# Cutting the first weight load and the last one of a decode kernel into row groups and single rows

## The chip, the cores and the metric

The kernel runs on one core of one Trainium2 chip. The metric is the device time of one execution in microseconds (us); medians and ranges over several executions are quoted. A profile covers one execution. Its span, from the first to the last instruction, is about 1.7 us shorter than the device time of the same execution (1342.8 and 1344.51 us for the kernel before).

Terms of the views: PE is TensorE, DVE is VectorE, ACT is ScalarE, and SPq is the SyncE queue that issues the loads. HBM is the memory that the loads read, SBUF the on-chip memory of 128 partitions that they write. The chain of waits starts from the last instruction and goes back, at each step, to what released it. "issue" is time in which an engine waited for nothing that the profile shows.

## The reference

One decode step for 4 sequences with one new token each: attention over an 8192-long cache with 32 heads, mixed with a gated feed-forward block. Cut to what matters:

```python
q = x @ wq                                # wq: 1024 x 4096, bf16, 8 MB
scores = q . k_cache * Dh ** -0.5         # k_cache: 4 x 32 x 8192 x 128, 268 MB
o = softmax(scores) . v_cache             # v_cache: the same size
a = o @ wo                                # wo: 4096 x 1024, 8 MB
b = x + sigmoid(r) * ((silu(x @ w_gate) * (x @ w_up)) @ w_down)
return g * a + (1 - g) * b
```

Nearly all the work is to read the two caches once.

## The kernel before

All loads are issued by the SyncE queue (SP) into a ring of five slots in SBUF, each 32 KB for each of 128 partitions. `load_pair` fills two slots with one DMA where they are neighbours. The first load is wq: row c of the view is partition c, with 64 KB.

```python
def load_pair(src, n, apart=False):
    a = slots(2)
    if a + 1 < NS and not apart:
        lo = a * RING
        nc.sync.dma_start(out=flat[:, lo:lo + 2 * n], in_=src)
        return [flat[:, lo:lo + n], flat[:, lo + n:lo + 2 * n]]
    # ... two DMAs where the slots are not neighbours

N = H * Dh
wq_at = load_pair(A_wq.rearrange("(c t) n -> c (t n)", t=DT), DT // 2 * N)
# ... small loads of x, w_r and gate_w, then w_gate, K, V ...
```

A pass after scheduling, `begin_early`, moves the first DMA of the program ahead of the barrier at which the engines meet on entry. At the other end the last loads are blocks of wo. Each block is four rows of 1024 for each partition. The last two blocks are loaded in halves, so that TensorE can begin on a half:

```python
last = [wo_block(g) for g in range(2, NWB - 2)]
last += [wo_block(g, r, r + FR // 2) for g in (NWB - 2, NWB - 1) for r in (0, FR // 2)]
# ... each use() is two matmuls (one for each half of the output) for every row
```

## Time and profile before

| | before |
|---|---|
| median time | 1344.42 us (1344.25 to 1344.47, 3 runs) |
| profiled span | 1342.8 us |
| PE busy / DVE busy | 77% / 46% of the span |
| chain of waits, DMA's share | 65% |
| first load (wq) issued / landed | 0.00 / 22.1 us |

The page's slices cut the span into 40 equal parts of 33.6 us. "DMA" is the busy share of the 16 DMA engines in tenths, "GB/s" what they moved.

```profile
DMA  9999999999999999999999999999999999999997
GB/s 414 434 434 430 432 436 430 444 433 418 445 430 424 440 431 425 437 436 432 432 438 431 426 433 430 434 436 435 432 423 441 430 427 431 436 426 443 423 423 331
```

The DMA engines are full from the first slice to the last. So I reckon that time lost at the start of the stream is not won back later, and that time after the last landing is added.

The chain of waits of the first 80 us (start us, length us, what):

```profile
1.46 20.99 DMA x<-in_gate_w_dram
...
23.48 3.63 PE S_ps L313 x32
27.11 0.02 issue
27.13 0.33 SPq L198
27.45 16.35 another core or an unknown queue
43.81 0.02 issue
43.82 34.94 DMA ring<-in_A_k_cache_dram
```

The tiny loads of x, w_r and gate_w queue behind wq, so that they land at 22.4 us. TensorE computes q; that frees a slot for the second half of the first K load (27.13 us). The load after that is issued at 43.82 us. By the order of the ring it waits for a slot of w_gate; the chain does not name what released it. The loads in the queue bridge these waits.

The first PE groups in the timeline (start us, busy us, what; in brackets the idle time before and what ended it):

```profile
22.58 0.63 PE L226 MATMUL small<-identb,x 6*128 6x6 bf16 x8 [22.58 <-DMA x<-in_gate_w_dram]
23.48 5.36 PE L313 MATMUL S_ps<-ring,xw 128*4 128x512 bf16 x64 [0.28 <-DVE xw L228]
...
39.34 5.97 PE L313 MATMUL o_ps<-ring,xw 128*4 128x512 bf16 x56 [4.99 <-DMA ring<-in_B_w_gate_dram]
```

The end of the chain of waits, and the last PE groups of the timeline:

```profile
1323.81 15.04 DMA ring<-in_A_wo_dram
1338.85 0.04 issue
1338.89 1.04 PE acc L279 x4
1339.93 0.02 issue
1339.95 0.57 ACT TB L590
```

```profile
1333.72 3.71 PE L279 MATMUL acc<-ring,LT 128*4 128x512 bf16 x16 [0.33 <-DMA ring<-in_A_wo_dram]
1337.66 1.02 PE L279 MATMUL acc<-ring,LT 128*4 128x512 bf16 x4 [0.23 <-DMA ring<-in_A_wo_dram]
1338.89 1.02 PE L279 MATMUL acc<-ring,LT 128*4 128x512 bf16 x4 [0.21 <-DMA ring<-in_A_wo_dram]
```

TensorE waits about 0.2 us for each of the last two halves, and four matmuls follow the last landing.

The trace also records every packet of the load queue. The kept records do not name the engine. I put the wq packets in order of their start and cut them into rounds of 16, one for each DMA engine:

```
wq before, 64 KB packets: starts (us)   duration (us): mean, min, max
round 1                   1.01 to 1.80  3.20  2.89  3.44
round 2                   4.11 to 4.71  2.42  2.42  2.42
... (rounds 3 to 7: means 2.42 to 2.53)
round 8                  18.61 to 19.38 2.42  2.42  2.42    last end 21.79
```

After the first round a packet of 65,536 bytes takes 2.42 us in nearly every case, which is 27.1 GB/s for an engine, or 433 GB/s for 16.

### The profile page before, as it was taken

The page shows a single profiled execution, that of the slowest core. Times are in us where ns is not written, and L with a number is a line of the kernel's source. Part 1 is how long each engine was busy: PE and PEld are TensorE (multiplying, and loading weights), DVE is VectorE, ACT ScalarE, POOL GpSimd, SP SyncE. Part 2 cuts the span into 40 slices and gives each one's busy share as a digit, 9 for nine tenths or more (in the row PEclk, how much of TensorE's full clock was granted, in tenths as well). Part 3 has the DMA queues.
Part 4 walks back from the last instruction along what each step waited for, and adds up shares of the span by engine and source line. Part 5 has one row for each costly group of instructions (what it writes and reads, how often), then busy time and mean ns, then how long its engine had stood idle before and what let it go on. Part 6 is the DMA issues. An engine that isn't in the chain of part 4 may idle for free.

```text
span 1342.8 us, 7621 instructions
## 1 busy us (share of the span) xinstructions
PE 1033.8 (77%) x4536; PEld 226.1 (17%) x2348; DVE 612.4 (46%) x358; ACT 50.6 (4%) x46; POOL 55.3 (4%) x90
## 2 busy tenths in 40 slices
PE   2665877787788687778987779598778679877897
PEld 0111111111111111111211112111111112111221
DVE  2555655544346554335455546146555244556000
ACT  0000100001000010001000010000100010000100
POOL 2000010001000010001000010000100010000100
PEclk9687988988999898889888889898889799889799
DMA  9999999999999999999999999999999999999997
GB/s 414 434 434 430 432 436 430 444 433 418 445 430 424 440 431 425 437 436 432 432 438 431 426 433 430 434 436 435 432 423 441 430 427 431 436 426 443 423 423 331
DMA packets 14172, 576.18 MB, mean 429 GB/s; under 512 B 1582, under 2 KB 1590, under 8 KB 2108
## 3 DMA queue, kind: packets, MB, share of 16 engines
q1 hardware_dynamic: 14132, 575.69, 99.5%
q8 instruction: 27, 0.44, 0.1%
q14 instruction: 5, 0.04, 0.0%
q10 hardware_dynamic: 8, 0.00, 0.0%
HBM read 575.68 MB, written 0.01 MB: 429 GB/s over the span
## 4 chain that ended last, share of the span: by engine, by line
DMA 65%; DVE 20%; PE 12%; another core or an unknown queue 1%; ACT 0%; issue 0%; SPq 0%; DVEq 0%
DMA ring<-in_A_k_cache_dram 56%; DVE TB L443 20%; PE o_ps L523 10%; DMA ring<-in_A_v_cache_dram 7%; DMA x<-in_gate_w_dram 2%; DMA ring<-in_A_wo_dram 1%; PE S_ps L449 1%; ACT PB L494 0%; PE S_ps L313 0%; PE acc L313 0%; PE small L543 0%; ACT OS L535 0%; PE acc L279 0%; DVE OS L536 0%
## 5 line engine op out<-in xcount | busy, mean ns | idle before, releaser
L443 DVE STREAM_TRANSPOSE TB<-ring 128x2048 uint32<-128x2048 uint32 x256 | 567.3, 2278 | 495.2 <-DMA ring<-in_A_k_cache_dram 493.9
L449 PE MATMUL S_ps<-TB,Z 128*128 128x512 bf16 x2048 | 520.0, 409 | 218.7 <-DVE TB L443 218.5
L523 PE MATMUL o_ps<-ring,PB 128*32 128x512 bf16 x2048 | 461.9, 389 | 52.5 <-DMA ring<-in_A_v_cache_dram 47.9
L449 PEld LDWEIGHTS <-Z 128*128 128x128 bf16 x1024 | 105.5, 103 | 628.8 <-issue 627.3
L523 PEld LDWEIGHTS <-PB 128*32 128x32 bf16 x1024 | 100.9, 99 | 410.0 <-issue 401.3
L536 DVE SCALAR_TENSOR_TENSOR OS<-o_ps,mE,OS 128x512 f32<-128x512 f32 x8 | 6.0, 751 | 104.1 <-ACT OS L535 104.1
L474 ACT ACTIVATE PTs<-S_ps,negm 128x1024 bf16<-128x1024 f32 x8 | 8.9, 1114 | 1024.9 <-DVE negm L471 1024.9
L425 POOL TENSOR_TENSOR Z<-qa,mq 128x16 bf16<-128x16 bf16 x32 | 9.1, 286 | 744.4 <-PE S_ps L449 654.7
L496 POOL COPY PB<-PT 32x1024 bf16<-32x1024 bf16 x16 | 30.4, 1903 | 82.1 <-PE o_ps L523 81.7
L494 ACT COPY PB<-PT 32x1024 bf16<-32x1024 bf16 x16 | 30.5, 1907 | 1.5 <-DVE PT L476 1.3
L376 DVE CAST LT<-small 128x64 bf16<-128x64 f32 x2 | 0.5, 225 | 40.6 <-PE small L374 40.6
L226 PE MATMUL small<-identb,x 6*128 6x6 bf16 x8 | 0.6, 197 | 22.6 <-DMA x<-in_gate_w_dram 22.6
L467 POOL PARTITION_ALL_REDUCE gmx<-mex x8 | 3.2, 396 | 340.7 <-DVE mex L464 340.7
L462 DVE TENSOR_REDUCE m<-S_ps 128x1 f32<-128x1024 f32 x8 | 9.8, 1225 | 15.9 <-PE S_ps L449 15.9
L279 PE MATMUL acc<-ring,LT 128*4 128x512 bf16 x64 | 15.0, 378 | 2.0 <-DMA ring<-in_A_wo_dram 1.4
L476 DVE STREAM_TRANSPOSE PT<-PTs 128x1024 bf16<-128x1024 bf16 x8 | 10.0, 1245 | 10.2 <-ACT PTs L474 10.2
L279 PE MATMUL acc<-ring,hT 128*4 128x512 bf16 x56 | 12.2, 379 | 0.0
L535 ACT ACTIVATE OS<-o_ps,mE 128x512 f32<-128x512 f32 x8 | 5.5, 687 | 158.8 <-PE o_ps L523 158.8
L313 PE MATMUL o_ps<-ring,xw 128*4 128x512 bf16 x56 | 6.0, 555 | 5.0 <-DMA ring<-in_B_w_gate_dram 5.0
L543 PEld LDWEIGHTS small<-selg,OS 128*128 128x128 f32 x64 | 9.0, 208 | 4.1 <-issue 3.9
L543 PE MATMUL small<-selg,OS 128*128 128x16 f32 x64 | 8.7, 269 | 0.0
L548 DVE SCALAR_TENSOR_TENSOR OT<-small,sgb,rinv 128x16 bf16<-128x16 f32 x8 | 1.8, 225 | 10.5 <-PE small L543 10.5
(71 smaller groups left out, 67.1 us busy)
## 6 DMA issues: line engine op xcount, KB each, us to landing
ring<-in_A_k_cache_dram SPq DMA_DIRECT2D x14, 4096.0 KB
ring<-in_A_v_cache_dram SPq DMA_DIRECT2D x14, 4096.0 KB, 31.2
ring<-in_B_w_gate_dram SPq DMA_DIRECT2D x1, 7168.0 KB, 37.6
ring<-in_B_w_up_dram SPq DMA_DIRECT2D x1, 7168.0 KB, 39.2
ring<-in_B_w_down_dram SPq DMA_DIRECT2D x2, 3584.0 KB, 27.5
ring<-in_A_wo_dram SPq DMA_DIRECT2D x6, 1024.0 KB, 21.0
ring<-in_A_v_cache_dram SPq DMA_DIRECT2D x2, 2048.0 KB, 26.8
ring<-in_A_v_cache_dram SPq DMA_DIRECT2D x4, 1024.0 KB, 25.0
```

The source lines that it names most:

```text
L279: nc.tensor.matmul(out_ap, lhsT=lhsT, rhs=rhs, start=start, stop=True, skip_group_check=True)
L313: nc.tensor.matmul(ps[32 * k:32 * k + Bn, z, :], lhsT=xT[TW * half + t], rhs=cols(w, t, 4 * z + k), start=(half + t == 0), stop=(half == 1 ...
L425: nc.gpsimd.tensor_tensor(out=Z[:, :, QP - 1:QP - 1 + P].rearrange("p e (q c) -> p e q c", c=QP)[:, :, :, 0], in0=qa[:, :, h0:h0 + NQ, b], ...
L443: nc.vector.transpose(out=flat_t.bitcast(U32), in_=kn[:, c * CJ * Dh:(c + 1) * CJ * Dh].bitcast(U32))
L449: nc.tensor.matmul(sps[:, z, :], lhsT=Z[:, he, s:s + P], rhs=T[:, 16 * z:16 * z + 16, half, :, e], start=(t == 0 and n == 0 and he == 0), ...
L462: nc.vector.tensor_reduce(out=m1[:], in_=sps[:].rearrange("p z n -> p (z n)"), axis=AX.X, op=ALU.max)
L474: nc.scalar.activation(out=PTs[:], in_=sps[:].rearrange("p z n -> p (z n)"), func=ACT.Exp, bias=negm[:, 0:1], scale=scale, accum_out=rs[:, ...
L476: nc.vector.transpose(out=PT[:].rearrange("p j i -> p (j i)"), in_=PTs[:])
L494: nc.scalar.copy(out=Bv[at, :, :, q, :], in_=Pv[at])
L496: nc.gpsimd.tensor_copy(out=Bv[at, :, :, q, :], in_=Pv[at])
L523: nc.tensor.matmul(o_ps[row:row + NM, e, :], lhsT=PB[:, RD * t + c, z, w].rearrange("p e s j -> p (e s j)"), rhs=vn[:, j0 * Dh:(j0 + 4) * ...
L543: nc.tensor.matmul(oT[:, :], lhsT=o_sb[:, q * Dh:(q + 1) * Dh], rhs=selg[:, q].rearrange("p t s -> p (t s)"), start=(q == 0), stop=(q == 3))
```

## The change

The intent has two parts. At the start, a smaller first load could let every DMA engine get its first packet sooner: 16 rows, one for each engine, go ahead of the barrier, and the other 112 rows follow it. At the end, a smaller last load leaves TensorE less work after the last landing.

```diff
-    def load_pair(src, n, apart=False):
+    def load_pair(src, n, p0=0, p1=P, apart=False):
...
-            nc.sync.dma_start(out=flat[:, lo:lo + 2 * n], in_=src)
+            nc.sync.dma_start(out=flat[p0:p1, lo:lo + 2 * n], in_=src)
...
-    wq_at = load_pair(A_wq.rearrange("(c t) n -> c (t n)", t=DT), DT // 2 * N)
+    wqv = A_wq.rearrange("(c t) n -> c (t n)", t=DT)
+    wq_at = load_pair(wqv[0:16], DT // 2 * N, 0, 16)
+    turn[0] = 0
+    load_pair(wqv[16:P], DT // 2 * N, 16, P)
...
-    last += [wo_block(g, r, r + FR // 2) for g in (NWB - 2, NWB - 1) for r in (0, FR // 2)]
+    cuts = [(NWB - 2, 0, 2), (NWB - 2, 2, 4), (NWB - 1, 0, 2), (NWB - 1, 2, 3), (NWB - 1, 3, 4)]
+    last += [wo_block(*cut) for cut in cuts]
```

Not a byte more is loaded. The instructions differ only by two more DMAs.

## The prediction

> **What bounds the kernel.** The DMA stream. The page's slices show DMA at 9 tenths in 39 of 40 slices and 429 GB/s on average; the chain of waits is 65% DMA. PE is busy 77%, DVE 46%. In the trace, a 64 KB packet of the load queue takes 2.42 us (27.1 GB/s), so 576 MB over 16 engines is 1328 us of an 1342.8 us span. A delay of the stream's start, or of the tail after its last landing, counts in full.
>
> **Start.** The first load (wq, 128 rows of 64 KB) is issued at 0.00 us, ahead of the barrier. Its first packets start 1.0 to 1.8 us later, spread over the engines, and take 2.9 to 3.4 us instead of 2.42; the landing is at 22.1 us. Issuing 16 rows first, one per engine, should only narrow the spread: at most about 0.4 us gained. The 112 rows follow at about 0.8 us.
>
> **The cost I expect.** The Trainium skill, "SBUF — State Buffer", section on the DMA port swizzle, says that DMA bandwidth follows the number of SBUF ports that a transfer's partitions reach: partitions 0 to 15 reach 4 of 16 ports, measured there at 104 GB/s for 1 MiB. The skill's "DMA: Bandwidth & Descriptors", on why a DMA increments its semaphore by 16, gives a DMA of 16 or 112 rows 16 engines, so each engine has one row, four engines on a port. No run here shows this; before has only 128-row loads at 27.1 GB/s per engine. If it holds, the first 16 packets take 4 x 2.42 = 9.7 us rather than 3.2: about 7 us lost. The 112 rows, 7 per engine, no longer pair each engine with one port. If each engine takes 7 neighbouring rows, sharing the ports evenly, I estimate (2.42 us a packet) that engines finish wq at 29 to 36 us and, after the next 128-row load, are 7 to 17 us late; the slowest decides at the end. Before's landings of one transfer spread over 1 us at the start but 6 us late in the run, so some of the skew may fall on engines that are otherwise ahead: I count +13 us in all.
>
> **Tail.** Before, the last wo half lands at 1338.85 us, four matmuls take 1.02, ACT's copy 0.57, then the output goes out. With a one-row last transfer two matmuls follow the last landing: about 0.43 us saved. Against it, 2 KB packets (0.084 us each against 0.159 for 4 KB, so slightly dearer) and one more completion: below 0.15 us. Net -0.3 us.
>
> **Sum.** 1344.4 + 13 - 0.4 = 1357 us. Range 1343.5 to 1364. Faster by over 2%: 0.00; within 2%: 0.93; slower by over 2%: 0.07.
>
> **What would show it.** First 16 packets of the load queue at about 9 to 10 us each; landing of the small x loads and start of the q matmuls moved from 22.4 to 30 us or more, the gate matmuls from 39.3 by 7 to 17 us; wider landings of the early loads; the rest of the span shifted but unchanged in shape; two matmuls, not four, after the last landing.
>
> **What would make it wrong.** If each row's engine is set so that the ports do not collide, or a port takes more than one engine's rate, the first packets keep about 3 us and the result is 1343.5 to 1344.3 us. If only the first 16 rows collide, about +7 us. If neighbouring rows go to different engines in all of the 112 rows, so four engines share a port throughout, the loss could reach tens of us and pass 2%.

## The result, and the profile after

| | before | after |
|---|---|---|
| median time | 1344.34 us (1344.12 to 1344.47, 4 runs) | 1365.69 us (1363.96 to 1366.9, 4 runs) |
| ratio, 95% interval | | 1.0158 (1.0143 to 1.0173) |
| profiled span | 1342.8 us | 1362.2 us |

A ratio is the mean time of one kernel's fast runs over that of the other's of the same rounds, so it is not quite the ratio of the medians. The changed kernel is 1.6% slower, which is within 2% but clear of noise, and above the range that I had given.

The slices after:

```profile
DMA  9999999999999999999999999999999999999998
GB/s 216 380 436 440 428 433 430 433 433 435 430 435 425 440 431 423 438 433 426 445 435 420 439 435 430 430 429 435 437 431 436 432 420 445 430 424 436 425 427 333
```

"DMA" says 9 tenths as before, yet the first slice moves 216 GB/s instead of 414. The engines are busy and slow. From the third slice on there is no difference. The chain of waits at the start:

```profile
0.79 42.70 DMA ring<-in_A_wq_dram
43.49 0.14 issue
43.63 3.62 PE S_ps L316 x32
47.25 0.02 issue
47.27 0.33 SPq L198
47.59 17.35 another core or an unknown queue
64.94 0.02 issue
64.96 34.24 DMA ring<-in_A_k_cache_dram
```

The wait for the landing of wq now stands where the wait for the tiny loads stood. From the q matmuls on it has the same steps as before, and the K load that was issued at 43.82 us is issued at 64.96, or 21.1 us later. The PE groups of the timeline moved by the same amount (39.34 to 60.47 us for w_gate):

```profile
41.90 0.63 PE L229 MATMUL small<-identb,x 6*128 6x6 bf16 x8 [41.90 <-DMA x<-in_gate_w_dram]
43.63 5.69 PE L316 MATMUL S_ps<-ring,xw 128*4 128x512 bf16 x64 [1.09 <-DMA ring<-in_A_wq_dram]
...
60.47 1.88 PE L316 MATMUL o_ps<-ring,xw 128*4 128x512 bf16 x16 [5.67 <-DMA ring<-in_B_w_gate_dram]
```

The end of the chain of waits, and the last PE group:

```profile
1341.34 16.08 DMA ring<-in_A_wo_dram
1357.42 0.04 issue
1357.46 1.90 PE acc L282 x8
1359.36 0.02 issue
1359.39 0.57 ACT TB L594
```

```profile
1353.73 5.62 PE L282 MATMUL acc<-ring,LT 128*4 128x512 bf16 x24 [0.34 <-DMA ring<-in_A_wo_dram]
```

The view merges the last 24 matmuls into one group, but one short wait is left in it. By the single records the 17th starts 0.49 us after the 16th, where the others follow at 0.21 to 0.22; in the kernel before, the two waits show as steps of 0.61 and 0.59 us. Eight matmuls follow this wait, so the landing that the chain names (1357.42 us) is that of a half, not of the last row; for the single rows TensorE does not wait.

The packet records, in rounds as above:

```
wq after, 64 KB packets: starts (us)    duration (us): mean, min, max
round 1 (the 16 rows)     1.01 to 1.72  8.59  7.98  9.33    last end 10.46
round 2 (of the 112)      9.00 to 10.46 5.29  5.03  5.72
round 3                  14.72 to 15.46 4.68  4.65  4.75
round 4                  19.39 to 20.12 3.11  2.73  4.65
round 5                  22.48 to 24.75 3.78  3.63  4.46
round 6                  26.16 to 28.38 4.55  4.20  4.81
round 7                  30.36 to 33.09 4.71  4.58  4.85
round 8                  35.11 to 37.66 4.49  4.32  4.84    last end 42.50
```

wq is in 20.7 us later than before (42.50 - 21.79), which is nearly the whole loss of 21.4 us between the medians. The two profiled executions themselves differ by less: the last packet of the load queue ends 19.9 us later (1358.29 us, before 1338.43), and the span is 19.4 us longer. So about 0.8 us of the delay was won back along the stream there. The first round was foreseen. What was not foreseen is that in rounds 2, 3, 6, 7 and 8 all 16 engines, not only some, take nearly two packet times.

### The profile page after: what moved, and what is told of

Same layout as the page of the kernel before. It is cut to its first block, busy times and chain, and to the rows that moved or that the text cites. A ratio compares the mean times of both kernels' runs of the same rounds, so it can differ in the third digit from the quotient of the medians.

```text
span 1362.2 us, 7625 instructions
## 1 busy us (share of the span) xinstructions
PE 1031.8 (76%) x4536; PEld 225.8 (17%) x2348; DVE 612.0 (45%) x358; ACT 50.6 (4%) x46; POOL 55.1 (4%) x90
## 4 chain that ended last, share of the span: by engine, by line
DMA 66%; DVE 20%; PE 12%; another core or an unknown queue 1%; ACT 0%; issue 0%; DVEq 0%; SPq 0%
DMA ring<-in_A_k_cache_dram 58%; DVE TB L446 20%; PE o_ps L526 9%; DMA ring<-in_A_v_cache_dram 4%; DMA ring<-in_A_wq_dram 3%; PE S_ps L452 2%; DMA ring<-in_A_wo_dram 1%; ACT PB L497 0%; PE S_ps L316 0%; PE small L546 0%; PE acc L316 0%; PE acc L282 0%; ACT OS L538 0%; DVE OS L539 0%
```

## The experiments

Theory P (ports): the loss comes from which partitions a transfer covers. By the Trainium skill, "SBUF — State Buffer", section on the DMA port swizzle, 128 partitions lie on 16 DMA ports, and the ports that a range reaches set its rate. The port counts in the expectations below come from the map in that section. I call a port crowded when two or more engines write to it at the same time. Rivals: theory S (source), that the neighbouring rows in HBM, read together, are slow; theory C (count), that a further DMA, or a small one ahead of the barrier, costs in itself. Twelve kernels ran, all with right results.

### One part alone: the tail

The edit is the `cuts` lines of the change, with wq as before.

> Tail part of the change alone (wq in one 128-row load as before). If the whole loss is in the wq split, this is 1344.0 us, 0.2 to 0.5 us under before. If the extra DMA, or its shift of the semaphore rotation, costs something through the run, it is above 1345.

Measured: 1343.7 us (1343.56 to 1344.07, 5 runs) against 1344.19 (1344.07 to 1344.37, 9 runs). The interval of the ratio (0.9984 to 1.0009) includes 1, so 0.5 us is a tendency, though four of the five runs are under every run of before. The tail is not the loss. The end of its chain of waits is that of the changed kernel:

```profile
1337.60 0.04 issue
1337.64 1.90 PE acc L279 x8
1339.55 0.02 issue
1339.57 0.57 ACT TB L591
```

PE is done at 1339.55 us instead of 1339.93. In this trace, too, the 17th of the last 24 matmuls starts late (0.51 us after the 16th).

### One part alone: the wq split

The edit is the wq lines of the change, with the tail as before.

> The wq split alone, tail as before. If the loss is all in the split: 1365 to 1367 us, about 21.5 us over before, with the wq packets as in the full change (8.6 us each for the first 16, then mostly 4.5 to 5.3). If the two parts interact, it differs from the full change by more than 1 us.

Measured: 1364.55 us (1364.12 to 1367.0, 4 runs), ratio 1.0155. The packets of the first round take 8.48 us on average, and wq's last packet ends at 42.22 us. The whole loss is in the wq split. The median is 0.45 us under the range that I expected and 1.1 us under that of the full change, just past the 1 us that I had set as the sign of an interplay. Each kernel varies by about 3 us and the two ranges overlap, so the runs neither show an interplay nor rule out a small one.

### The same first megabyte, cut by columns

```diff
-    wq_at = load_pair(A_wq.rearrange("(c t) n -> c (t n)", t=DT), DT // 2 * N)
+    wqv = A_wq.rearrange("(c t) n -> c (t n)", t=DT)
+    slots(2)
+    nc.sync.dma_start(out=flat[:, 0:N], in_=wqv[:, 0:N])
+    nc.sync.dma_start(out=flat[:, N:DT * N], in_=wqv[:, N:DT * N])
+    wq_at = [flat[:, 0:DT // 2 * N], flat[:, DT // 2 * N:DT * N]]
```

> The same idea cut the other way: the first load is 128 rows of 8 KB (the same 1 MB), the second 128 rows of 56 KB; tail as before. Port theory (cost comes from which partitions a transfer covers): every engine keeps its own port, packets run at 27 GB/s, wq lands at about 22 us, total 1344 +-0.7 us. Count theory (a second, or a small first, DMA ahead of the barrier costs time in itself): well above 1346.

Measured: 1343.92 us (1343.83 to 1344.42, 5 runs) against 1344.19, ratio 0.9998. Two DMAs with the small one ahead of the barrier cost nothing when both cover 128 partitions, so theory C falls. The intended gain at the start is too small to be told from none: the first packets start at 1.00 to 1.47 us, before at 1.01 to 1.80.

### wq in two halves of 64 rows

```diff
+    wqv = A_wq.rearrange("(c t) n -> c (t n)", t=DT)
+    slots(2)
+    for p in (0, P // 2):
+        nc.sync.dma_start(out=flat[p:p + P // 2, 0:DT * N], in_=wqv[p:p + P // 2])
... (load_pair of wq is dropped; wq_at as in the column cut)
```

> wq in two loads of 64 rows. Port theory: 64 rows reach 8 of 16 ports and 4 neighbouring rows go to each engine, so two engines share a port in every step: 8 packets of 4.84 us each, wq lands at about 40 us, total about +19.4 us, 1363.8 us. If instead the odd number of rows per engine (7) was what hurt, 4 rows per engine cost little: under 1350 us.

Measured: 1365.57 us (1365.41 to 1365.79, 4 runs), ratio 1.0158. There is no odd number of rows here, and the loss is the same. In seven rounds of eight, all packets take 4.98 to 5.13 us (the first, 4.72 to 5.33). The view by stretches has from, to and length in us, then each engine's busy time, the granted clock, the DMA share and GB/s:

```profile
20.00:30.00 10.00, 0.00 (x0) 0.00 (x0) 0.00 (x0) 0.00 (x0) 0.76 (x1) 1.00 1.01 210
30.00:40.00 10.00, 0.00 (x0) 0.00 (x0) 0.00 (x0) 0.00 (x0) 0.00 (x0) 1.00 1.02 210
```

The DMA engines are full (1.01 and 1.02; packets are put down to one stretch as a whole, hence over 1) at half the rate. The skill's section gives about 218 GB/s for 64 partitions; 16 packets of 64 KB in 5.12 us are 205 GB/s. My figure of 19.4 us was 2 us short, because the packets took 5.12 us each and not 2 x 2.42.

### An extra load of 16 rows

To measure the two terms apart, the next kernels keep before's wq load and put an extra load ahead of it. It goes to ring space that is overwritten afterwards. Where the gate load overlaps that space it waits for the extra load, with wq queued in the meantime. The cuts after the first show only the line of the extra load.

```diff
+    wqv = A_wq.rearrange("(c t) n -> c (t n)", t=DT)
+    nc.sync.dma_start(out=flat[0:16, 3 * RING:3 * RING + DT * N], in_=wqv[0:16])
     wq_at = load_pair(A_wq.rearrange("(c t) n -> c (t n)", t=DT), DT // 2 * N)
```

> Before, plus an extra 16-row load of wq (1 MB, partitions 0 to 15, into ring space that is overwritten later; result stays right) ahead of the unchanged 128-row load. Port theory: its packets take 8 to 9.3 us as in the changed kernel, then the 128-row load runs at full speed: wq done 8.1 us later than before, total 1352.5 us (1351.5 to 1353.5). The other 13 us of the loss would then belong to the 112 rows. If the 16 rows alone upset everything behind them, nearer 1365.

Measured: 1353.8 us (1353.54 to 1353.96, 4 runs) against 1344.35: +9.4, where 8.1 was expected. The first round takes 8.41 us a packet and the next 3.90; then all are at 2.42. The total is 0.3 us above my range: the crowding spilled over into one further round, and no more.

### The same megabyte over 128 partitions

```diff
+    nc.sync.dma_start(out=flat[:, 3 * RING:3 * RING + N],
+                      in_=wqv[0:16].rearrange("r (q n) -> (r q) n", q=DT))
```

> As the extra 16-row load, but the same 1 MB of the same addresses in HBM is spread over 128 partitions of 8 KB. Port theory (destination): 2.4 us of stream and no more, 1346.8 us (1346 to 1347.6). Source theory (16 neighbouring rows in HBM are slow to read together): as slow as the 16-row one, about 1352.5 us.

Measured: 1346.59 us (1346.41 to 1346.8, 4 runs), +2.2. The same bytes from the same addresses cost 7.2 us less when they are written to all partitions. That is the first term of the loss, and theory S falls for the 16 rows.

### The 16 rows written with a step of 7 partitions

```diff
+    nc.sync.dma_start(out=flat[16:122:7, 3 * RING:3 * RING + DT * N], in_=wqv[0:16])
```

> As the extra 16-row load, but to partitions 16, 23, 30 ... 121: what 16 engines would write in the first step of the 112 rows if each took 7 neighbouring rows. They reach 14 ports; only 2 ports have two engines, the other 12 engines have a port alone. Free-running engines: 12 packets of about 3.2 us, 4 of about 5. Coupled engines (a crowded port holds up all): all 16 packets at about 5 us, as in the second round of packets in the changed kernel. Total 1347 to 1350 us.

Measured: 1349.24 us (1348.98 to 1349.38, 4 runs), +4.9. The first-round packets, sorted, in us:

```
4.04 4.19 4.20 4.20 4.27 4.28 4.29 4.43 4.43 4.44 4.47 4.51 4.59 4.74 4.74 4.88
```

By the skill's port map 12 of these 16 engines have a port to themselves. None of them ran at the 2.9 to 3.4 us that a first packet takes in before, so with two crowded ports all 16 were slow. This kernel differs from the extra load to partitions 0 to 15 only in the partitions that it writes, and it is 4.6 us faster (1353.8 - 1349.24). So the 16 packets of 64 KB are not what is slow in themselves.

### The 16 rows read from far apart

```diff
+    nc.sync.dma_start(out=flat[0:16, 3 * RING:3 * RING + DT * N], in_=wqv[0:P:8])
```

> As the extra 16-row load to partitions 0 to 15, but read from every eighth row of wq (512 KB apart). Port theory: the same as with neighbouring rows, packets of 8 to 9.3 us, 1352.5 us. Source theory: much faster, 1347 us.

Measured: 1353.3 us (1353.17 to 1353.47, 4 runs), +9.0; first-round packets 7.84 to 9.15 us. Moving the source changes 0.5 us, moving the destination 7.2.

### One crowded port instead of two

```diff
+    nc.sync.dma_start(out=flat[3:109:7, 3 * RING:3 * RING + DT * N], in_=wqv[0:16])
```

> As the extra 16-row load with a step of 7, but starting at partition 3 (3, 10, 17 ... 108): by the port map 15 ports are reached and only one has two engines. If one crowded port holds up all engines: all packets at 4 to 4.9 us as with two crowded ports, total 1349.2 us. If it takes two crowded ports, as the quick third round of 64 KB packets in the changed kernel suggests (14 packets of about 3 us, two of 4.65): 14 packets near 3.2 us, two near 4.7, total about 1347.5 us.

Measured: 1348.02 us (1347.91 to 1349.02, 4 runs), +3.7. Fourteen packets took 3.18 to 3.80 us, two took 4.40 and 6.01. With one crowded port most run nearly free; with two they do not. The total lies between my two figures.

This also reads the rounds of the changed kernel. If each engine takes 7 neighbouring rows of the 112, the port map gives, step by step, 2, 2, 1, 1, 2, 2 and 2 crowded ports. The two rounds with one crowded port are exactly the quick ones (means of 3.11 and 3.78 us; the others take 4.49 to 5.29).

### The 112 rows alone, and the same bytes over 128 partitions

```diff
+    nc.sync.dma_start(out=flat[16:P, 3 * RING:3 * RING + DT * N], in_=wqv[16:P])
```

> Before, plus an extra load of the 112 rows to partitions 16 to 127 (7 MB, overwritten later, result right) ahead of the unchanged 128-row load, with no 16-row load at all. If the 112 rows are slow by themselves, as in the changed kernel (32.0 us from the last end of the first round to their end), total +32 us or a little less: 1374 to 1377 us. If they were slow only because they followed the crowded 16 rows: +17 to +20 us.

```diff
+    nc.sync.dma_start(out=flat[:, 3 * RING:3 * RING + 7 * N],
+                      in_=A_wq[16 * DT:D].rearrange("(p s) n -> p (s n)", s=7))
```

> The same 7 MB of the same HBM addresses as an extra load over 128 partitions of 56 KB. Port theory: 16.9 us of stream, 1361.3 us (1360.5 to 1362.5). Source theory: as slow as the 112-row form, 1374 to 1377 us. The difference of the two kernels, expected 14 to 15 us, is the second term of the loss.

Measured: 1374.67 us (1373.97 to 1375.55, 4 runs) for the 112 rows, +30.4, and 1361.14 us (1361.05 to 1361.25, 4 runs) for the same bytes over 128 partitions, +16.9. The difference, 13.5 us, is the second term of the loss. It needs no 16-row load ahead of it, and it is not in the addresses that are read. The rounds of the 112 rows have the same pattern here: means of 3.53 and 3.28 us in the two rounds with one crowded port, 4.37 to 4.77 in the other five. The step-of-7 loads, which read other rows of wq, give nearly the same with one round each (3.66 us with one crowded port, 4.42 with two), so the partitions written are enough to explain the rounds. The stretch of each extra load in the view by stretches, first the 112 rows, then the spread form:

```profile
2.00:32.00 30.00, 0.00 (x0) 0.00 (x0) 2.35 (x3) 0.07 (x1) 8.68 (x21) 1.00 0.94 240
```

```profile
2.00:18.00 16.00, 0.00 (x0) 0.00 (x0) 2.35 (x3) 0.08 (x1) 4.99 (x20) 1.00 0.94 405
```

At the same busy share, 0.94, the 112 rows move at 240 GB/s and the spread form at 405.

### The column cut and the one-row tail together

> The column cut of wq and the one-row tail together, each of which was slightly under before alone (-0.3 and -0.5 us). If they add: 1343.4 us (1343.2 to 1343.8). If one makes the other idle: 1343.7 to 1344.

Measured: 1343.77 us (1343.49 to 1344.29, 5 runs) against 1344.28 (1344.11 to 1344.47, 9 runs), ratio 0.9996 (0.9984 to 1.0009). It is no better than the tail alone. The runs do not show the two to add, and neither gain is clear of the interval.

## Why the prediction was wrong

- **What bounds the kernel: right.** A delay of the stream's start counted nearly in full: in the profiled executions wq was 20.7 us later, the K load behind it was issued 21.1 us later, and the span was 19.4 us longer, with about 0.4 us saved by the tail (19.9 - 19.4); the medians differ by 21.4 us.
- **The first 16 rows: right, the size in part by luck.** About 7 us lost was predicted; the extra loads give 9.4 - 2.2 = 7.2 us. Packets of 9 to 10 us were expected; they took 8.0 to 9.3 (7.6 to 9.1 in the extra load). The round behind them, for which no loss was reckoned, took 3.90 us a packet instead of 2.42 in the extra load's kernel. The two errors nearly cancel.
- **The 112 rows: this step failed.** The prediction said "If each engine takes 7 neighbouring rows, sharing the ports evenly, I estimate (2.42 us a packet) that engines finish wq at 29 to 36 us and, after the next 128-row load, are 7 to 17 us late". The assignment of rows fits the runs, but the engines do not run freely. Where two ports were crowded, all 16 packets were slow, those on a port of their own too (4.04 to 4.88 us, step of 7). The engines finished wq at 39.6 to 42.5 us, and after the next 128-row load they were 19.5 to 20.9 us late (the last 16 packet ends of each kernel, paired in order of time).
- **The discount for skew: failed with it.** "some of the skew may fall on engines that are otherwise ahead: I count +13 us in all" needs engines that are unequally late. They were late nearly alike (19.5 to 20.9 us), so there was little skew to absorb. As a term of the sum: 13 us less 7 for the 16 rows leaves 6 us for the 112 rows; they measured 13.5.
- **The sum closes.** 7.2 + 13.5 = 20.7 us, against 20.4 us between the medians for the split alone.
- **The tail: right in size (-0.3 predicted, -0.5 us measured, not clear of noise), not in detail.** Eight matmuls, not two, follow the last landing that TensorE waits for, and from there its own pace of 0.21 to 0.22 us a matmul ends the kernel.
- **The gain at the start: not seen.** At most 0.4 us was allowed; the column cut measured 0.3 us with an interval that includes none.

Left open: why two crowded ports hold up all engines when one does not (the number of crowded ports fits every round of the 112 rows, but no trace names the port of a packet); why the two kernels with the 16 and 112 row split vary by 3 us between runs where before varies by 0.4; and the gains of the tail and the column cut, too small for five runs.

## What to carry to other kernels

Cut a load that feeds all 128 partitions along its columns rather than along its partitions: the 1 MB ahead of the barrier cost nothing as 128 rows of 8 KB and 7 us as 16 rows of 64 KB. When a transfer crowds two ports or more, reckon all its packets at the crowded rate rather than each engine at its own; with one crowded port, 14 of 16 packets ran nearly free here. A DMA share of 9 tenths does not mean a good rate: read the GB/s line beside it.

## What the Trainium skill lacked or had wrong

- "SBUF — State Buffer", the DMA port swizzle: it gives rates by the number of ports that a range reaches, but not how crowded ports slow the engines that have a port of their own. ("DMA: Bandwidth & Descriptors" tells of a full port that holds up other engines too, but only for remote DMA between cores and without a rate.) Sixteen rows that reach 14 ports all took 4.04 to 4.88 us a packet, while with 15 ports 14 of 16 took 3.18 to 3.80.
- "SBUF — State Buffer", the same section: about 218 GB/s is given as the limit for 64 partitions; loads of 64 rows of 64 KB ran at 205 GB/s (16 packets of 64 KB in 5.12 us).
- "DMA: Bandwidth & Descriptors", on why a DMA increments its semaphore by 16: it says how many engines a DMA of 112 rows gets, but not which rows each gets. The rounds fit 7 neighbouring rows each (two quick rounds, 3.11 and 3.78 us, where that gives one crowded port).
- "DMA: Bandwidth & Descriptors", rules for kernel authors: it advises against two transfers to disjoint partition halves because they serialize, and gives no cost there; the rate for 64 partitions stands in the other page. In the run the same 8 MB took about twice as long, 21 us more in all.
